# Two kinds of DMA writes change places between ScalarE's queue and SyncE's

## The chip, the cores and the metric

The kernel runs on one core of a Trainium2 chip. The metric is the device time of one execution in microseconds, the median of several; lower is better.

## The reference

The program is linear attention followed by a layer of eight experts. For each of 8 batches and 8 heads, `kv = k^T v` (64 x 64) over 576 positions, `out = q kv`, and each row of 64 is divided by its root mean square and multiplied by `g_norm`. The heads side by side are the rows `x` (4608 tokens x 512). Then

```python
logits = x @ w_gate
e_idx = argmax(logits, axis=1)
gate_w = probs[arange(N), e_idx]            # softmax of logits
eom = sigmoid(x @ w_output_gate)
for e in range(8):
    mask = e_idx == e
    h = maximum(x[mask] @ w1[e], 0)         # 512 -> 1024
    out[mask] = gate_w[mask, None] * eom[mask, e, None] * (h @ w2[e])
```

All of it is float32; the kernel splits float32 operands of the large products into a high and a low part.

## The kernel before

**Tiles and groups.** The 4608 tokens are 36 tiles of 128. Tiles 0 to 15 are the early ones (`EARLY = 16`), 16 to 35 the late ones. They also form four groups of 9, 7, 10 and 10 tiles (`GR`); the first two groups are the early tiles. `kv_part` makes a batch's kv product (kvps, L586), `kvT_part` and `m_part` fold the gate weights into it, `out_tile` multiplies a tile's q with it (ops, L665) and evicts the result: on ScalarE the raw row `xrow` (L674), the squares `sq` (L677) and the gate sums `gp` (L696). Two tiles share one row buffer of 512 KB. When the second of the pair is evicted, `write()` sends the buffer to DRAM (`xs`) through `xwrite` (L1064), 18 times in all: 8 for early tiles and 10 for late ones.

**Row buffers.** Loads of k, v and q (L549) and row buffers of the late part come from one pool of eight slots, `xfree`. `load` fills it with loads until one slot is left. `take` hands out the slot that has been free longest, and `give` puts a slot back as soon as its write has been issued; the next user waits for that write to land.

**Norms and routing.** `route` runs once for each group: the inverse norms of the rows (`xtail`, L760), the logits, the argmax, the rank of each token in its expert, and the tables of token numbers. `xtail` holds 16 numbers a token, eight inverse norms and one scale for the output. The early groups write their norms at once to `xr` (L763, L765). The rest of their scales, `rest_of_scales`, is left for later: the first layer steps it three times (at f = 1, 2, 3), and its third step issues the write of `xtail` to `xt` on ScalarE's queue (L865), for both early groups. The late groups write theirs through `xwrite`.

**Experts.** `run(i)` does one layer pass: `mm1` in eight blocks f (hps, L405: 12 matmuls each), whose result ScalarE evicts with a Relu (hT, L413) and VectorE makes a low part of (L415); two buffers of hps alternate, so block f + 2 waits for VectorE's work on block f. Then `mm2` for each tile of 128 tokens (yps, L441: 24 matmuls), evicted with the output scale from `tl` (y, L453) and scattered to `out` (L454). Weights are loaded in pieces of 512 KB on SyncE's queue (wraw, L220, `wload`) and split on ScalarE (whi, L256 and L263) and VectorE (wlo, L259 and L266). GpSimd gathers token rows (`xg`) and their norms and scales (`tl`, L283) by index. The first eight passes use early tokens only (256 for each expert), the later ones the rest.

**Order.** The order on every engine and queue is written out by hand (`manual_schedule`). Work of the late tiles is a generator, `late`, of which one step is taken after each block of a layer (`unit`); so kvps, ops and their evictions stand between the blocks of the first passes. `early()` is the time up to the first layer, about 66 us. After it `late_open[0]` is set to True and the first late pair (tiles 16 and 17) is finished; the pairs after it follow in the first passes, up to about 190 us. In the first pass, the block f = 3 is followed by the weights' load `wload(1, 1, 1)`, then by the third step of `rest_of_scales` and then by a step of `late`.

**Queues.** SyncE's queue issues all loads and all rows; ScalarE's queue stands in ScalarE's own order of instructions, so a DMA issue that must wait holds all of ScalarE's work behind it.

Of the kernel before, what the change touches and what calls it, by code (L numbers as in the profile page):

```python
# [153 lines left out]
def body(ctx: ExitStack, tc: tile.TileContext, kvm, rem, qT, wg, gn, w1, w2, kc, xs, xr0, xr, xt, tab, out):  # L154
    nc = tc.nc
# [35 lines left out]
    held = {}  # L191
# [8 lines left out]
    def give(t):  # L200
        i = held.pop(id(t))[0]
        (free if i < SLOTS else xfree).append(i)
# [73 lines left out]
    def rows_of(dram, g0, n):  # L276

        r0, w, t = (EARLY, EARLY, g0) if g0 < EARLY else (XE, LATE, g0 - EARLY)
        return dram[r0:r0 + P * w].rearrange("(m s) x -> m s x", s=w)[:, t:t + n]
# [140 lines left out]
    def mm2(i, k, events):  # L420
# [31 lines left out]
        else:  # L452
# [21 lines left out]
    xtail = c1.tile([P, NT, TW], F32, name="xtail")  # L474
# [3 lines left out]
                        in_=xtail[:, 0:w // TW, :].rearrange("p n x -> p (n x)"))  # L478
# [29 lines left out]
    for i in range(2):  # L508
        o = c1.tile([P, GMAX + 1, E], BF16, name=f"ohb{i}")
# [129 lines left out]
    def out_tile(g, later=False):  # L639
# [45 lines left out]
        def write():  # L685
            xwrite(c0, rows_of(xs, c0, k), x)
# [35 lines left out]
    def route(gi):  # L722
# [5 lines left out]
        n = len(GROUPS[gi])  # L728
        last = gi + 1 == len(GROUPS)
        g0 = GROUPS[gi][0]  # L730
# [30 lines left out]
        rows_ = rows_of(xt, g0, n)  # L761
# [8 lines left out]
        def scaled(j):  # L770
            w = j.stop - j.start
            eng = nc.gpsimd if gi < EARLY_GROUP and j.start else vec
            eng.tensor_tensor(out=gpv[:, :, j], in0=gpv[:, :, j],
                              in1=rv.unsqueeze(2).to_broadcast([P, n, w, E]), op=ALU.mult)

        def summed(j):
            return vec.tensor_reduce(out=lg[:, :n, j], in_=gpv[:, :, j], axis=AX.X, op=ALU.add)
# [50 lines left out]
        def gate():  # L828
            vec.tensor_tensor(out=og[:, :n], in0=oh[:, :n], in1=lg[:, :n, E:2 * E], op=ALU.mult)
            yield 0  # L830
            vec.tensor_reduce(out=ogs[:, :n], in_=og[:, :n], axis=AX.X, op=ALU.add)
            yield 0
            vec.tensor_scalar(out=ogs[:, :n], in0=ogs[:, :n], scalar1=-88.0, scalar2=None, op0=ALU.max)

        def exps():
            nc.scalar.activation(ex[:, :n], d[:, :n], AF.Exp)
            nc.scalar.activation(eo[:, :n], ogs[:, :n], AF.Exp, scale=-1.0)

        def norm(k):
            if k == 0:  # L840
                vec.tensor_reduce(out=se[:, :n], in_=ex[:, :n], axis=AX.X, op=ALU.add)
            elif k == 1:
                vec.tensor_scalar(out=eo[:, :n], in0=eo[:, :n], scalar1=1.0, scalar2=None, op0=ALU.add)
            else:
                vec.tensor_scalar(out=se[:, :n], in0=se[:, :n], scalar1=1e-9, scalar2=None, op0=ALU.add)

        def scales():
            vec.reciprocal(dn[:, :, :n], dn[:, :, :n])
            yield 0
            vec.tensor_tensor(out=xtail[:, g0:g0 + n, C_SCALE], in0=se[:, :n], in1=eo[:, :n], op=ALU.mult)  # L850

        def rest_of_scales():
            if lead:
                scaled(halves[1])
                summed(halves[1])
            for _ in gate():
                pass
            yield
            exps()
            for k in range(3):  # L860
                norm(k)
            for _ in scales():
                pass
            yield
            nc.scalar.dma_start(out=rows_, in_=xtail[:, g0:g0 + n])  # L865
            yield

        early = g0 < EARLY
# [113 lines left out]
        if not early:  # L982
            yield from scales()
            xwrite(g0, rows_, xtail[:, g0:g0 + n])
# [27 lines left out]
        elif not lead:  # L1012
            tps, acc = table_part(0, TMAX)
            yield from pause(9)
            if not gi:
                nc.scalar.copy(gix0, tps[:, 0, 0:1])
                gather_row(0, 0)
            vec.tensor_copy(acc, tps)
            scales_late.append(rest_of_scales())
        else:  # L1020
            tps, acc = table_part(0, TA, rl)
# [15 lines left out]
            tick[0] = None  # L1037

            scales_late.append(rest_of_scales())

            def others():
# [13 lines left out]
    issued = []  # L1055
    issue_mark = c1.tile([P, 1], F32, name="issue_mark")
    xwrites = []
    opened = [False]

    def xwrite(g, o, i):  # L1060
        if not opened[0]:
            xwrites.append((g, o, i))
            return
        nc.sync.dma_start(out=o, in_=i)  # L1064
        if id(i) in held:
            give(i)

    def open_rows():
        opened[0] = True
        for w in list(xwrites):  # L1070
            xwrite(*w)
        xwrites.clear()
# [195 lines left out]
            step()  # L1268
            yield

    late_open = [False]
    vec = nc.vector
    ce = cf[:, K_E:K_E + E]
    perm = cst.tile([P, E, E], F32, name="perm")
# [257 lines left out]
    with ExitStack() as p3:  # L1532
# [4 lines left out]
        with tc.For_i(0, nreg) as i:  # L1537
# [36 lines left out]
            for f in range(8):  # L1574
                ph = pt.tile([P, P], F32, name="oph")
                for d in range(4):
                    o = d * 256 + (f % 2) * P
# [3 lines left out]
            for f in range(8):  # L1581
# [5 lines left out]
                                         in_=y, in_offset=None, bounds_check=NTOK - 1, oob_is_err=False)  # L1587


def build():  # L1590
    nc = bacc.Bacc("TRN2", target_bir_lowering=False, num_devices=1)

    def inp(name, shape, dt=F32):
        return nc.dram_tensor(name, shape, dt, kind="ExternalInput").ap()

    kvm = inp("kvm", (B, P, 4, 2, DM))
    rem = inp("rem", (B // 2, P, 2, DM))
    qT = inp("qT", (NTOK // QC, P, NP, QC))
    wg = inp("wg", (P, 2, 4 * E))
    gn = inp("gn", (P, 1))  # L1600
    w1 = inp("w1", (E, 4, P, 1024))
    w2 = inp("w2", (E, 4, P, 1024))
    kc = inp("kc", (P, K_N))
    out = nc.dram_tensor("out", (NTOK, DM), F32, kind="ExternalOutput").ap()
    xs = nc.dram_tensor("xs", (XR, DM), F32).ap()
    xr0 = nc.dram_tensor("xr0", (XE, TW), F32).ap()
    xr = nc.dram_tensor("xr", (XE, TW), F32).ap()
    xt = nc.dram_tensor("xt", (XR, TW), F32).ap()
    tab = nc.dram_tensor("tab", (P, NOVER), F32).ap()
    with tile.TileContext(nc) as tc:  # L1610
        body(tc, kvm, rem, qT, wg, gn, w1, w2, kc, xs, xr0, xr, xt, tab, out)
    return nc
# [27 lines left out]
```

## Time and profile before

| what | us |
|---|---|
| median of 3 runs (582.49 to 587.55) | 582.75 |
| the profiled execution's own time | 582.92 |
| its span, first to last instruction | 581.0 |
| TensorE busy in the span | 557.4 |
| VectorE, ScalarE, GpSimd busy | 344.3, 286.2, 221.6 |
| mean granted TensorE clock | 0.994 |

The time is the span and about 2 us around it. Rows of the profile name an engine (PE is TensorE, PEld its weight loads, DVE is VectorE, ACT is ScalarE, POOL is GpSimd, SP is SyncE; a q behind the name means that the engine's sequencer issues or waits), a line of the kernel, an operation, and what it writes and reads. A granted clock of 1.00 is 2.4 GHz and 0.50 is 1.2 GHz.

### The profile page before, as it was taken

Reading aid. Unit: us, or ns where it says so; the run is one execution under the profiler, and the core shown is the slowest. Engines: PE = TensorE matmul, PEld = TensorE weight load, DVE = VectorE, ACT = ScalarE, POOL = GpSimd, SP = SyncE. Lnnn points to the kernel's source line nnn. Section 1 sums busy time; section 2 is a strip of 40 time slices with the busy share of each in tenths; the row PEclk is TensorE's granted clock in tenths of the full one; section 3 lists DMA queues with packets and bytes.
Section 4 is the critical chain, followed back from the end, with each engine's and each line's share of the span. In section 5 each row is a group of like instructions: output and inputs, shape, how many; then the busy total and the mean of one; then the engine's idle time right before and its main releaser. Section 6 shows DMA issues by size and latency. Waiting matters only on the chain.

```text
span 581.0 us, 11889 instructions
## 1 busy us (share of the span) xinstructions
PE 557.4 (96%) x4643; PEld 478.0 (82%) x4643; DVE 344.3 (59%) x635; ACT 286.2 (49%) x486; POOL 221.6 (38%) x204
## 2 busy tenths in 40 slices
PE   7998997999999999999999999999999999999995
PEld 3775786898988898888979889889897988888894
DVE  2268555565587989877595746445355363646450
ACT  1355346566666656746563434535344444535440
POOL 4343333332313251533565326235262453545202
PEclk9999999999999999999999999999999999999998
DMA  8999799986966485666855445346454645556200
GB/s 306 418 417 368 244 415 361 321 309 248 313 221 232 157 307 199 197 231 207 273 188 195 130 146 156 118 152 211 146 179 142 202 162 156 176 170 207 75 6 38
DMA packets 38794, 126.31 MB, mean 217 GB/s; under 512 B 6940, under 2 KB 8333, under 8 KB 38736
## 3 DMA queue, kind: packets, MB, share of 16 engines
q1 hardware_dynamic: 29664, 105.26, 52.5%
q0 software_dynamic: 8352, 19.88, 10.1%
q8 instruction: 38, 0.62, 0.4%
q10 hardware_dynamic: 720, 0.39, 0.2%
q14 instruction: 20, 0.16, 0.1%
HBM read 106.01 MB, written 20.04 MB: 217 GB/s over the span
## 4 chain that ended last, share of the span: by engine, by line
PE 76%; DMA 9%; DVE 5%; issue 4%; ACT 3%; POOL 1%; ACTq 0%; POOLq 0%; SPq 0%; DVEq 0%
PE hps L405 32%; PE yps L441 31%; PE ops L665 4%; DMA ld<-qT 3%; DMA ld<-kvm 3%; PE tps L350 3%; PE yps L435 3%; PE kvps L586 2%; DVE wlo L266 2%; DMA wgs<-wg 1%; ACT whi L263 1%; PE cps L558 1%; DVE wlo L259 1%; DVE hT L415 1%; DMA xs<-xrow 1%
## 5 line engine op out<-in xcount | busy, mean ns | idle before, releaser
L405 PE MATMUL hps<-xT,whi 128*128 128x256 f32 (+8 forms) x992 | 214.2, 308 | 3.6 <-DVE hT L415 2.2
L441 PE MATMUL yps<-whi,hT 128*128 128x512 f32 (+3 forms) x592 | 200.7, 402 | 0.0
L405 PEld LDWEIGHTS hps<-xT,whi 128*128 128x128 f32 x992 | 163.9, 190 | 10.1 <-DVE hT L415 3.9
L405 PE MATMUL hps<-xT,wlo 128*128 128x256 f32 (+8 forms) x496 | 150.8, 304 | 0.0
L441 PEld LDWEIGHTS yps<-whi,hT 128*128 128x128 f32 (+3 forms) x592 | 111.0, 187 | 24.5
L441 PE MATMUL yps<-wlo,hT 128*128 128x512 f32 (+3 forms) x296 | 116.7, 394 | 0.0
L415 DVE SCALAR_TENSOR_TENSOR hT<-hps,hT 128x256 fp32r<-128x256 f32 (+9 forms) x168 | 62.9, 394 | 90.5 <-ACT hT L413 81.1
L454 POOL DMA_INDIRECT out<-y,oidx x42 | 45.5, 1084 | 178.2 <-ACT y L453 143.2
L413 ACT ACTIVATE hT<-hps 128x256 fp32r<-128x256 f32 (+8 forms) x128 | 55.1, 430 | 116.0 <-PE hps L405 107.8
L259 DVE SCALAR_TENSOR_TENSOR wlo<-wraw,gcol,whi 128x1024 fp32r<-128x1024 f32 x62 | 83.4, 1347 | 44.6 <-ACT whi L256 43.0
L266 DVE TENSOR_TENSOR wlo<-wraw,whi 128x1024 fp32r<-128x1024 f32 x64 | 84.3, 1317 | 25.7 <-ACT whi L263 22.3
L405 PEld LDWEIGHTS hps<-xT,wlo 128*128 128x128 f32 x496 | 94.0, 189 | 0.3
L256 ACT ACTIVATE whi<-wraw,gcol 128x1024 fp32r<-128x1024 f32 x62 | 71.3, 1151 | 0.6 <-DVE wlo L266 0.6
L317 POOL TENSOR_TENSOR xg<-xg,tl 128x512 f32<-128x512 f32 (+8 forms) x41 | 48.3, 1178 | 54.3 <-DMA tl<-xt,gidx 39.6
L283 POOL DMA_INDIRECT xg<-xs,gidx x41 | 46.7, 1140 | 53.6 <-PE hps L405 33.1
L263 ACT CAST whi<-wraw 128x1024 fp32r<-128x1024 f32 x64 | 66.6, 1041 | 0.0
L283 POOL DMA_INDIRECT tl<-xt,gidx x41 | 53.3, 1300 | 30.1 <-PE hps L405 18.3
L441 PEld LDWEIGHTS yps<-wlo,hT 128*128 128x128 f32 (+3 forms) x296 | 55.6, 188 | 10.4
L453 ACT ACTIVATE y<-yps,tl 128x512 f32<-128x512 f32 (+3 forms) x37 | 25.4, 687 | 60.3 <-PE yps L441 48.3
L353 ACT CAST xT<-tps 128x512 fp32r<-128x512 f32 (+8 forms) x42 | 23.0, 548 | 44.6 <-PE tps L350 43.5
L357 DVE TENSOR_TENSOR xT<-tps,xT 128x512 fp32r<-128x512 f32 (+8 forms) x42 | 26.6, 636 | 20.4 <-ACT xT L353 20.1
L665 PE MATMUL ops<-aug,ld 64*64 64x80 f32 (+1 forms) x960 | 32.1, 244 | 3.8 <-ACT gp L696 3.0
(184 smaller groups left out, 444.3 us busy)
## 6 DMA issues: line engine op xcount, KB each, us to landing
wraw<-w SPq DMA_DIRECT2D x128, 512.0 KB
ld<-kvm SPq DMA_DIRECT2D x32, 512.0 KB
ld<-qT SPq DMA_DIRECT2D x18, 512.0 KB
xs<-xrow SPq DMA_DIRECT2D x18, 512.0 KB
ld<-rem SPq DMA_DIRECT2D x4, 512.0 KB
out<-y,oidx POOLq DMA_INDIRECT x42
xg<-xs,gidx POOLq DMA_INDIRECT x41
tl<-xt,gidx POOLq DMA_INDIRECT x41
```

Source lines behind the costliest of these rows:

```text
L256: he.activation(hi, r, AF.Copy, scale=gcol[:, 0:1])
L259: eng.scalar_tensor_tensor(out=lo, in0=r, scalar=gcol[:, 0:1], in1=hi.bitcast(F32), op0=ALU.mult, op1=ALU.subtract)
L263: he.copy(hi, r)
L266: eng.tensor_tensor(out=lo, in0=r, in1=hi.bitcast(F32), op=ALU.subtract)
L283: return nc.gpsimd.indirect_dma_start(out=o[:M, :], out_offset=None, in_=dram[0:XE] if i < E else dram, in_offset=bass.IndirectOffsetOnAxi ...
L317: return eng.tensor_tensor(out=v, in0=v, in1=f, op=ALU.mult)
L405: seq.append(nc.tensor.matmul(ps[:, :C], w[:, o:o + P], x[d][:, :C], start=(d == 0 and k == 0), stop=(d == 3 and k == 2)))
L413: nc.scalar.activation(h[:, 0:C], ps[:, :C], AF.Relu)
L415: nc.vector.scalar_tensor_tensor(out=h[:, l:l + b - a], in0=ps[:, a:b], scalar=0.0, in1=h[:, a:b].bitcast(F32), op0=ALU.max, op1=ALU.subtract)
L441: seq.append(nc.tensor.matmul(ps[:M], a, b, start=(f == 0 and n == 0), stop=(f == 7 and n == 2)))
L454: i_ = nc.gpsimd.indirect_dma_start(out=out, out_offset=bass.IndirectOffsetOnAxis(ap=oidx[i // E][:M, RUNS[i][0], t:t + 1], axis=0), in_=y ...
L665: nc.tensor.matmul(ps[c0:c0 + step_, u, p * W:(p + 1) * W], qt[g // 2][r, p, q0:q0 + step_], augs[b % 3][r, p, :], start=True, stop=True)
```

## The change

The third step of `rest_of_scales` issues its write on SyncE's queue instead of ScalarE's (two writes, one for each early group). `xwrite` asks two things: has `late_open` been set, and is the tensor in the table `held` of slots that are in use. If both hold, the write goes on ScalarE's queue, else on SyncE's as before. `late_open` is made earlier in the text, since `xwrite` now reads it. Nothing else differs: the order of the steps, the slots and the data stay.

```diff
@@ rest_of_scales @@
             yield
-            nc.scalar.dma_start(out=rows_, in_=xtail[:, g0:g0 + n])
+            nc.sync.dma_start(out=rows_, in_=xtail[:, g0:g0 + n])
             yield
@@ before xwrite @@
-    opened = [False]
+    opened, late_open = [False], [False]
 
     def xwrite(g, o, i):
         if not opened[0]:
             xwrites.append((g, o, i))
             return
-        nc.sync.dma_start(out=o, in_=i)
+        (nc.sync if late_open[0] is False or id(i) not in held else nc.scalar).dma_start(out=o, in_=i)
         if id(i) in held:
             give(i)
@@ after late @@
-    late_open = [False]
     vec = nc.vector
```

## Rows read from the trace of the kernel before

**Rows 1.** The page's first part: busy us, share of the span, instructions.
```profile
PE 557.4 (96%) x4643; PEld 478.0 (82%) x4643; DVE 344.3 (59%) x635; ACT 286.2 (49%) x486; POOL 221.6 (38%) x204
```

**Rows 2.** Stretches: length, busy us of PE, PEld, DVE, ACT, POOL, clock, DMA, GB/s.
```profile
80.00:90.00 10.00, 7.77 (x114) 6.59 (x109) 4.79 (x16) 4.26 (x10) 3.13 (x4) 1.00 0.99 382
90.00:100.00 10.00, 7.35 (x96) 5.90 (x97) 5.21 (x9) 5.33 (x12) 4.45 (x3) 0.98 1.01 368
...
99.00:104.00 5.00, 5.00 (x45) 3.99 (x38) 4.26 (x6) 4.82 (x8) 0.94 (x1) 0.66 0.97 387
110.00:180.00 70.00, 70.00 (x941) 60.83 (x940) 44.88 (x78) 43.73 (x83) 18.82 (x18) 1.00 0.79 277
```

**Rows 3.** TensorE's waits, 66 to 112 us: total us, times, longest.
```profile
PE kvps L586 <- issue: 1.1, 3, 0.4
```

**Rows 4.** TensorE's timeline: start, us, instructions, idle time before and its releaser.
```profile
88.23 0.50 PE L405 MATMUL hps<-xT,whi 128*128 128x256 f32 x2 [1.12 <-DVE hT L415]
...
90.90 0.51 PE L405 MATMUL hps<-xT,whi 128*128 128x256 f32 x2
...
98.75 0.79 PE L665 MATMUL ops<-aug,ld 64*64 64x80 f32 x32 [2.40 <-ACT gp L696]
```

**Rows 5.** ScalarE's timeline, from the first late pair to the first layer's end.
```profile
72.71 0.42 ACT L696 COPY gp<-ops 128x128 f32<-128x128 f32 x1
...
85.04 2.25 ACTq L865 DMA_DIRECT2D xt<-xtail  x2
87.33 0.38 ACT L413 ACTIVATE hT<-hps 128x256 fp32r<-128x256 f32 x1 [3.60 <-PE hps L405]
...
97.33 0.58 ACT L674 COPY xrow<-ops 128x512 f32<-128x512 f32 x1 [3.04 <-DMA xs<-xrow]
...
104.70 1.14 ACT L256 ACTIVATE whi<-wraw,gcol 128x1024 fp32r<-128x1024 f32 x1
```

**Rows 6.** The chain that ended last, 72 to 112 us: start, us, what.
```profile
73.48 11.48 DMA ld<-qT
```

**Rows 7.** SyncE's timeline: DMA issues from 67 to 104 us.
```profile
67.37 0.33 SPq L220 DMA_DIRECT2D wraw<-w  x1
67.77 1.30 SPq L549 DMA_DIRECT2D ld<-kvm  x2
69.19 3.46 SPq L220 DMA_DIRECT2D wraw<-w  x4
73.48 0.33 SPq L549 DMA_DIRECT2D ld<-qT  x1
75.36 0.33 SPq L1064 DMA_DIRECT2D xs<-xrow  x1
76.53 0.33 SPq L549 DMA_DIRECT2D ld<-qT  x1
77.80 0.33 SPq L220 DMA_DIRECT2D wraw<-w  x1
...
89.52 0.39 SPq L1064 DMA_DIRECT2D xs<-xrow  x1
...
92.33 4.06 SPq L220 DMA_DIRECT2D wraw<-w  x3
102.14 0.33 SPq L1064 DMA_DIRECT2D xs<-xrow  x1
```

**Rows 8.** Line L865: its instructions, ns min/median/max, first and last start.
```profile
L865 ACTq DMA_DIRECT2D xt<-xtail x2: 336/338/341, 85.0 to 86.9; - x2
```

**Rows 9.** GpSimd's timeline: gathers of norms and what waits for them.
```profile
79.20 0.94 POOL L283 DMA_INDIRECT tl<-xr,gidx  x1 [2.27 <-PE hps L380]
...
85.17 1.05 POOL L317 TENSOR_TENSOR xg<-xg,tl 128x512 f32<-128x512 f32 x1 [3.77 <-DMA tl<-xr,gidx]
...
93.37 0.99 POOL L283 DMA_INDIRECT tl<-xt,gix  x1 [0.15 <-PE kvTps L604]
```

**Rows 10.** TensorE's waits, 112 to 232 us: total us, times, longest.
```profile
PE ops L665 <- ACT gp L696: 0.6, 1, 0.6
```

## The prediction

> **What bounds the kernel now.** I read the page's busy times first, then the busy time by stretch, then TensorE's waits, then the chain and the queues at those places.
>
> TensorE is busy for 557.4 of 581.0 us [rows 1]: a change of queues can only give back idle time, or time at the lower clock. By stretch [rows 2], the reader is to see that 80 to 104 us is the weak place: TensorE is busy for 7.77 and 7.35 us of two stretches of 10, and then full at a lower clock; 110 to 180 us is full, at 1.00. The DMA share is near 1 at the weak place. Of the idle 4.88 us (2.23 + 2.65), 1.1 are unnamed waits of kvps [rows 3]; 1.12 us before hps at 88.23 are ended by VectorE's hT, and 2.40 before ops at 98.75 by ScalarE's gp [rows 4]; 0.26 are left in small gaps. Behind the 2.40 us the clock falls: from 99 to 104 us its mean is 0.66 [rows 2], so 5 x 0.34 = 1.70 us of work at 2.4 GHz are lost.
>
> Both idle times come from ScalarE, and both touch the change [rows 5]. At 85.04 its queue issues the two L865 writes, and hT L413, whose matmuls were over, starts at 87.33 after 3.60 us of idle time. At 97.33 the row copy L674 has waited 3.04 us for DMA xs<-xrow: the row buffers are run down to one spare, so a new pair of tiles gets the buffer that the pair before has just been written from, and waits for that write to land.
>
> Why L865 waits: the chain [rows 6] has a qT load ahead of it, issued at 73.48 and landed 11.48 us later, though L865 reads no qT. I read that an issue on either queue waits for the landing of the eighth issue before it. On SyncE's timeline [rows 7] qT of 73.48, the row write of 75.36, qT of 76.53 and the weights of 77.80 come one after the other, then four loads and the two L865; the first L865 has qT of 73.48 as its eighth in the program's order, the second the row write of 75.36. The second L865 goes at 86.95 (85.04 + 2.25 - 0.34, [rows 5, 8]), so landings come 1.9 us apart there, some 11 us behind their issue.
>
> **The two L865 writes go to SyncE's queue.** Removed from ScalarE: the 3.60 us. The fifth block's hT comes at about 84.1 instead of 87.33, and the 1.12 us before the seventh go, with the small gaps behind them. Added to SyncE: two issues of 0.34 us [rows 8] with the same kind of wait; behind them on that queue are loads, and no TensorE wait in this stretch is put down to a load. Cost there 0; if the loads came to be late, each held issue would cost TensorE up to the 1.9 us of one landing.
>
> What is late next is the norms' landing. They have landed by 93.37 now, when GpSimd's gather tl<-xt goes [rows 9]. Issued at some 85 us behind SyncE's backlog, they land at about 95. A gather of this kind took 5.97 us (79.20 to 85.17, [rows 9]), so tl lands at 101; ScalarE's y, which stands just ahead of the split at 104.70 [rows 5], would want it at about 100. That is a wait of 1 to 1.5 us on ScalarE while TensorE has the next tile's matmuls in the other buffer: cost 0, or some 2 us if the gather is 5 us later than I think.
>
> **The ten late row writes go to ScalarE's queue.** It is all ten: the flag is set before tile 17 is evicted, and their buffers are in the table that the new condition asks. The late groups' norms are not, and stay on SyncE.
>
> First, a write no longer stands behind SyncE's backlog. The second pair's took 7.8 us (89.52 to 97.33, [rows 5, 7]). 512 KB at the 368 to 387 GB/s of the stretch are 1.4 us, so 3 if it shares the engines with loads; between 3 and 7.8 I take 4, since its queue is empty. ScalarE comes to the next row copy at 93 to 94; a write issued by 90 has landed. So the 2.40 us go, and with them, likely, the 1.70 of the clock. Bounds: nothing of it (the write lands as late as now), or all 4.10.
>
> Second, the issue now stands in ScalarE's order with its wait. Queued behind it: hT, the split of w2, the next row; VectorE's hT waits for these, and TensorE for VectorE, two blocks later. Pair one is ready at 73.1 [rows 5]; its eighth issue before is the weights of 67.37, which released SyncE's row write at 75.36, or the load just ahead of them: held 2.2 us or 0. Of 2.2 us the 1.1 of unnamed idle time at 80 us would swallow half. I take 0, as ScalarE is ahead of SyncE here. Pair two counts: ready at about 86.8, its eighth issue before is qT of 76.53 in today's order, which lands at about 88.5 by the spacing of 1.9; if SyncE, no longer held by the row, comes one load ahead of it, it is the weights of 77.80, at 90.2. Held 1.7 or 3.4 us. Freed at 88.5 it costs the layer's last block, which would start at 89.3, nothing; freed at 90.2, 1.4 us. I take 0.5, nearer to today's order, and 0.4 for VectorE's kvc and the transposes behind the same wait. Pairs three to ten are free: the third is written at 102.14 [rows 7], 14 us behind its eighth, and landings took under 12.
>
> Third, ten issues of 0.34 us on ScalarE. From 110 to 180 us TensorE is busy for all 70.00 us with ScalarE at 43.73 [rows 2]: cost 0, and 2 us if none of it were covered. Beyond that, one wait for gp of 0.6 us [rows 10] lies near three issues: 0 to 1 us, I take 0.3. SyncE is rid of its waits for rows; weights come earlier, but TensorE does not wait for them: 0.
>
> **The sum.** 1.12 + 0.26 + 2.40 + 1.70 = 5.48 us gained, 0.5 + 0.4 + 0.3 = 1.2 given back: 4.3 us. From the profiled execution's 582.92 (span 581.0 and 1.9 around it) that gives 578.6; it is 0.17 above the median of the three runs, 582.75, so 578.5.
>
> The Trainium skill (DMA: Bandwidth & Descriptors, Issuing engines are not separate DMA queues) says that DMAs from SP, ACT and GpSimd run on the same 16 engines, so that spreading them saves issue time only. The trace agrees that they are full, at shares of 0.97 to 1.01. By that rule the row writes would bring nothing; the sum counts on the latency of one write, and not on rate.
>
> **Rivals.** *DMA is the bound.* What jumps the queue delays what it passes, and the next layer's weights land when they land. For: ScalarE's split at 104.70 uses weights issued at 92.33 [rows 5, 7], which land at 100 to 104 by the 7.8 and 11.48 us seen, so little can be gained at that point. Against: TensorE needs that split only at the next layer's fifth block. If it holds ScalarE, and the transposes behind it, some 1.7 us remain: 581.0; at the worst, nothing: 582.7. The skill's rule above is this rival.
>
> *ScalarE is held*, the slower side: the wait of pair two. If the eighth issue before is two or three loads further on, it lands at 92 to 94. This decides from 90.1 on: if ScalarE is freed later, the last block starts after its present 90.90 [rows 4], and each us costs TensorE one. Freed at 93 it starts at 93.8, 2.9 us late; kvc's chain adds 1.3, the clock falls as now, and of the savings 2.40 us stay: 584.5. Held to 97, with pair one held too, 588 to 589. For: a 3.60 us wait of this kind stands in the trace. Against: the order of issue, by which pair two counts back to a load made 10 us before.
>
> *The change doesn't do what it says:* with the row writes still on SyncE's queue, only L865's 1.38 us would go: 581.4. The code speaks against it.
>
> **How the numbers follow.** Forecast 0.57, its own range 577.2 to 580.3. DMA bound (with late tails and the change without effect) 0.18, at 581.0 to 582.7. ScalarE held 0.14, of which 0.07 above 588.6. More than 5.8 us gained, for which the 1.1 us at 80 us or waits behind 180 would have to go too, 0.11, at 576 to 577. The range 576.6 to 584.5 leaves out the long end of the held case and some of the last. A measurement of this kernel tells about 1% (5.8 us) from no change: faster by more 0.11, slower by more 0.07, within 0.82.
>
> **What would show it.** Right: no idle time of 2 us on ScalarE between 83 and 88; row writes that land within 5 us; no idle TensorE before ops at 94 to 98, and a granted clock of 1.00 from 99 to 104; everything behind 110 us some 4 us earlier. Wrong: ScalarE held for 3 us at the second row write, y waiting for tl, or the lower clock still there. If the stretches behind 110 us are no longer full, the loss is one I have not seen.

## The result, and the profile after

Before: 582.75 us, median. After: 590.3 us (589.48 to 592.15, five runs). The ratio is 1.0115, with a 95% interval of 1.0085 to 1.0144: slower by 1.15%, and clear of no change. Medians are of all runs and ratios of the runs as a whole without those in a slower state, some per cent longer at a lower granted clock, so that a ratio is not the quotient of two medians (here 1.0130). The profiled execution has a span of 588.4 us against 581.0, so 7.4 us are to be explained.

The stretches of [rows 2] and some behind them (columns as there), after the change:

```profile
70.00:80.00 10.00, 9.53 (x166) 9.13 (x170) 5.88 (x15) 5.83 (x15) 2.16 (x2) 1.00 1.00 389
80.00:90.00 10.00, 8.92 (x164) 7.78 (x156) 5.92 (x16) 4.36 (x11) 4.45 (x4) 1.00 1.03 415
90.00:100.00 10.00, 6.20 (x71) 4.90 (x63) 4.66 (x7) 5.09 (x10) 4.45 (x3) 1.00 1.03 416
...
99.00:104.00 5.00, 4.76 (x49) 3.85 (x50) 3.97 (x5) 5.00 (x10) 1.22 (x1) 1.00 0.97 296
110.00:180.00 70.00, 64.66 (x820) 55.86 (x819) 38.06 (x62) 38.12 (x73) 16.87 (x16) 0.95 0.70 246
...
130.00:140.00 10.00, 9.07 (x77) 7.17 (x78) 5.94 (x7) 6.61 (x14) 0.94 (x1) 0.83 0.74 260
160.00:170.00 10.00, 8.06 (x102) 7.33 (x102) 4.59 (x8) 6.64 (x15) 3.04 (x3) 0.83 0.65 242
```

The weak place gave nothing back in idle time: from 80 to 100 us TensorE is idle for 1.08 + 3.80 = 4.88 us, as before to the hundredth. Only the clock came back: 1.00 from 99 to 104 us, where it had been 0.66, worth the 1.70 us. The loss is where the row of before was full: from 110 to 180 us TensorE is idle for 70 - 64.66 = 5.34 us, and the clock has a mean of 0.95, which is 0.05 x 70 = 3.5 us of work, half of it in each of the two stretches at 0.83. With 0.47 us of idle time at 70 to 80 us the account is 5.34 + 3.5 + 0.47 - 1.70 = 7.6 us, for 7.4 measured.

TensorE's timeline after (columns as in [rows 4]) shows the idle times that fill most of this:

```profile
92.51 0.50 PE L405 MATMUL hps<-xT,whi 128*128 128x256 f32 x2 [2.40 <-DVE hT L415]
...
99.24 0.78 PE L665 MATMUL ops<-aug,ld 64*64 64x80 f32 x32 [1.03 <-ACT gp L696]
...
130.93 0.78 PE L665 MATMUL ops<-aug,ld 64*64 64x80 f32 x32 [3.28 <-ACT gp L696]
...
162.87 1.23 PE L665 MATMUL ops<-aug,ld 64*64 64x80 f32 x32 [1.94 <-ACT gp L696]
```

ScalarE's timeline after says why:

```profile
91.23 0.33 ACTq L1064 DMA_DIRECT2D xs<-xrow  x1
91.61 0.38 ACT L413 ACTIVATE hT<-hps 128x256 fp32r<-128x256 f32 x1 [4.16 <-DMA ld<-qT]
...
97.82 0.59 ACT L674 COPY xrow<-ops 128x512 f32<-128x512 f32 x1 [1.67 <-DMA xs<-xrow]
...
120.60 0.33 ACTq L1064 DMA_DIRECT2D xs<-xrow  x1
...
129.51 0.59 ACT L674 COPY xrow<-ops 128x512 f32<-128x512 f32 x1 [4.49 <-DMA xs<-xrow]
...
161.45 0.59 ACT L674 COPY xrow<-ops 128x512 f32<-128x512 f32 x1 [3.74 <-DMA xs<-xrow]
```

Two things are to be seen. At 91.23 the second pair's write holds ScalarE until a qT load lands: 4.16 us with the issue itself. It is the wait that stood at L865 in [rows 5], moved. And at 129.51 and 161.45 a row copy waits 4.49 and 3.74 us for the write before it, which has a queue of its own and was issued at once. In the chain of waits after (start, us, what) these writes are long:

```profile
72.98 6.94 DMA xs<-xrow
...
80.16 10.99 DMA ld<-qT
91.23 6.51 DMA xs<-xrow
...
120.60 8.84 DMA xs<-xrow
...
153.10 8.27 DMA xs<-xrow
```

What differs about the fourth pair's write (120.60) is best seen in SyncE's queue around it. Before the change, SyncE's timeline:

```profile
118.80 0.42 SPq L220 DMA_DIRECT2D wraw<-w  x1
121.62 0.33 SPq L1064 DMA_DIRECT2D xs<-xrow  x1
122.05 1.24 SPq L549 DMA_DIRECT2D ld<-kvm  x2
123.38 1.95 SPq L220 DMA_DIRECT2D wraw<-w  x2
```

and after it:

```profile
117.75 0.43 SPq L220 DMA_DIRECT2D wraw<-w  x1
118.27 1.91 SPq L549 DMA_DIRECT2D ld<-kvm  x2
120.28 1.42 SPq L220 DMA_DIRECT2D wraw<-w  x2
```

The four loads behind the row are the same. Before, SyncE stands for some 2.4 us (119.2 to 121.62) until the row is copied, issues it, and only then the loads. After, it goes on, and three of the four loads are out when ScalarE's queue issues the row at 120.60. The row copy of before that needs this write's buffer waits little for it, in ScalarE's timeline:

```profile
126.52 0.59 ACT L674 COPY xrow<-ops 128x512 f32<-128x512 f32 x1 [0.47 <-DMA xs<-xrow]
```

So the write took 126.52 - 121.62 = 4.9 us behind a queue that had paused, and 8.84 us on an empty queue beside one that had not.

The trace also has the packets of each DMA queue by stretch: packets, MB, and their share of the 16 engines. q1 is SyncE's queue, q10 ScalarE's and q0 GpSimd's. After the change, from the issue at 120.60 to 125.20 us:

```profile
q1 hardware_dynamic: 379, 1.39, 96.6%
```

and from 125.24 us until the write lands at 129.44:

```profile
q1 hardware_dynamic: 255, 0.95, 55.1%
q10 hardware_dynamic: 144, 0.52, 30.5%
q0 software_dynamic: 112, 0.27, 16.2%
```

The first packet of the write moves 4.64 us after the issue. Until then the engines move the loads of SyncE's queue; after it the queues share the engines for 4.2 us. More than half of the 8.84 us is the wait for the first packet. ScalarE's queue is not slow by itself: the writes that it issued at 180.44 and 194.24, when SyncE's queue had next to nothing under way, had their first packet after 0.84 and 0.83 us and their last after 2.53 and 2.45.

SyncE's waits before the change, 60 to 200 us (total us, times, longest), sum these pauses:

```profile
SPq L1064 <- ACT xrow L674: 39.9, 8, 6.7
```

They were not time that the loads could win. After the change SyncE stands no less in all, but most of it at the buffers of the weights and of the loads. At these two places it had been 7.2 and 7.9 us:

```profile
SPq L220 <- DVE wlo L266: 27.3, 6, 7.9
...
SPq L220 <- DVE wlo L259: 13.2, 4, 6.6
```

The loads behind a row leave a few us earlier, just ahead of its write, and then wait elsewhere.

### The profile page after: what moved, and what is told of

Its sections match the earlier page's. It is cut to its first block, busy times and chain, and to the rows that moved or that the text cites. A ratio compares the mean times of both kernels' runs of the same rounds, so it can differ in the third digit from the quotient of the medians.

```text
span 588.4 us, 11884 instructions
## 1 busy us (share of the span) xinstructions
PE 559.9 (95%) x4643; PEld 479.6 (82%) x4643; DVE 343.5 (58%) x635; ACT 286.5 (49%) x486; POOL 217.1 (37%) x204
## 4 chain that ended last, share of the span: by engine, by line
PE 75%; DMA 11%; DVE 5%; issue 4%; ACT 3%; POOL 1%; POOLq 0%; ACTq 0%; SPq 0%
PE yps L441 31%; PE hps L405 30%; DMA xs<-xrow 5%; PE ops L665 4%; PE tps L350 3%; PE yps L435 2%; PE kvps L586 2%; DMA ld<-qT 2%; DVE wlo L266 2%; DMA ld<-kvm 1%; DMA wgs<-wg 1%; PE cps L558 1%; ACT whi L263 1%; DMA tl<-xr,gidx 1%; ACT xrow L674 1%
## 5 line engine op out<-in xcount | busy, mean ns | idle before, releaser
L317 POOL TENSOR_TENSOR xg<-xg,tl 128x512 f32<-128x512 f32 (+8 forms) x41 | 45.5, 1110 | 52.5 <-DMA tl<-xt,gidx 38.3
L283 POOL DMA_INDIRECT tl<-xt,gidx x41 | 51.0, 1244 | 28.0 <-PE hps L405 18.2
```

The costliest lines, as they stand in the source:

```text
L283: return nc.gpsimd.indirect_dma_start(out=o[:M, :], out_offset=None, in_=dram[0:XE] if i < E else dram, in_offset=bass.IndirectOffsetOnAxi ...
L317: return eng.tensor_tensor(out=v, in0=v, in1=f, op=ALU.mult)
```

## The experiments

Theory one, the **backlog**: SyncE's waits for rows had kept the loads behind each row; without them the loads are ahead of the write on the DMA engines, on whatever queue it is. Its rival, **ScalarE held**: the issue in ScalarE's order holds ScalarE, and the rest follows from that. A second rival is that the **norms** on SyncE's queue do the harm. Ratios are to the kernel before on the same chip.

**One part alone.** The first kernel has the norms on SyncE's queue and all rows there too, the second the late rows on ScalarE's queue and L865 as before.

```diff
@@ norms_only, of the changed kernel @@
-        (nc.sync if late_open[0] is False or id(i) not in held else nc.scalar).dma_start(out=o, in_=i)
+        nc.sync.dma_start(out=o, in_=i)
@@ rows_only, of the changed kernel @@
-            nc.sync.dma_start(out=rows_, in_=xtail[:, g0:g0 + n])
+            nc.scalar.dma_start(out=rows_, in_=xtail[:, g0:g0 + n])
```

> Only the two L865 writes go to SyncE's queue; all rows stay there too. Theory (backlog: with the rows on ScalarE's queue SyncE no longer waits for them, issues loads ahead of them, and the writes land 6.5 to 8.9 us after their issue, so the next pair waits for its row buffer): this part is no cost. ScalarE's 3.60 us of idle time at 85 us go, the 1.12 us of TensorE too, the wait for ops near 98 us stays: 580 to 582 us. Rival (late norms: the gather of tl waits for norms behind SyncE's backlog and ScalarE's y waits for it): 583 us or more, with a ScalarE wait for tl near 100 us.

> Only the late rows go to ScalarE's queue; L865 stays there too. Backlog theory: the idle times before ops near 128 and 161 us of the changed kernel (3.28 and 1.94 us) and the two stretches of 3.4 us at half the clock are all there: 589 to 593 us. Rival (ScalarE held: the 4.16 us at the second row write are the cause): with L865 ahead of it the second write counts back to another issue, so its hold changes by over 1 us, and the time follows that hold and not the stalls near 128 and 161.

Norms alone: 584.96 us, ratio 1.0002 [0.9972, 1.0031], above the 580 to 582 us expected, and without the wait for tl that its rival named. Rows alone: 592.25 us, 1.0131 [1.0089, 1.0174], as expected and all of the loss. The norms on SyncE's queue do no harm, but bring nothing either, though ScalarE's 3.60 us and TensorE's 1.12 us of [rows 4, 5] are gone. SyncE's and ScalarE's timelines of the kernel with the norms alone say where that went:

```profile
88.83 0.86 SPq L865 DMA_DIRECT2D xt<-xtail  x2
90.37 0.54 SPq L1064 DMA_DIRECT2D xs<-xrow  x1
```

```profile
97.92 0.59 ACT L674 COPY xrow<-ops 128x512 f32<-128x512 f32 x1 [6.82 <-DMA xs<-xrow]
```

The second pair's row leaves SyncE's queue at 90.37, no earlier than the 89.52 of [rows 7], and the copy that waits for it starts 0.6 us later. ScalarE is ready for the buffer 3.2 us earlier (91.10 against 94.29) and waits 3.8 us longer (6.82 against 3.04).

In the kernel with the rows alone, ScalarE's hold at the second pair is 1.98 us instead of 4.16, but 3.82 us at L865 are back ahead of it, so ScalarE is held no less in all, and this run does not decide about that rival. TensorE's waits at 128 and 160 us are there (3.14 and 2.15 us). Its profiled execution shows no stretch at the lower clock there, so the clock's part differs between executions; the idle time doesn't.

**SyncE held again.** The rows stay on ScalarE's queue, but the first load behind each of them waits until the row has been copied, as SyncE's own issue had to.

`behind(d, x)` makes d wait for x; the issues of `wload` and `load` are wrapped in `held_back`, and `last_row` remembers the row copy L674.

```diff
@@ sync_held, of the changed kernel @@
+    hold = [None]
+
+    def held_back(d):
+        if hold[0] is not None:
+            behind(d, hold[0])
+            hold[0] = None
+        return d
...
-            nc.sync.dma_start(out=t, in_=src)
+            held_back(nc.sync.dma_start(out=t, in_=src))
...
-        (nc.sync if late_open[0] is False or id(i) not in held else nc.scalar).dma_start(out=o, in_=i)
+        on_act = late_open[0] and id(i) in held
+        (nc.scalar if on_act else nc.sync).dma_start(out=o, in_=i)
+        if on_act:
+            hold[0] = last_row[0]
```

> The changed kernel, but the first load that SyncE issues behind each late pair waits for that pair's second row copy, as SyncE did when it issued the row itself. Backlog theory: the fourth and sixth writes land in under 5.5 us instead of 8.84 and 8.27, the idle times before ops near 128 and 161 us fall below 0.7 us, the clock stays at 2.4 GHz there: 581 to 585 us. Rival (ScalarE's own queue is slow, whatever SyncE does): the writes still take 6.5 to 9 us, and the time stays at 588 us or above. Rival (ScalarE held): the hold of about 4 us at the second write stays, and with it 588 us or above.

581.76 us, as expected, ratio 0.9954 [0.9922, 0.9986], and 1.6% below the changed kernel's ratio, with the queue of every write as the change has it. ScalarE's timeline, and then TensorE's waits from 66 to 200 us:

```profile
90.06 0.33 ACTq L1074 DMA_DIRECT2D xs<-xrow  x1
90.44 0.38 ACT L421 ACTIVATE hT<-hps 128x256 fp32r<-128x256 f32 x1 [3.72 <-DMA wraw<-w]
...
119.41 0.36 ACTq L1074 DMA_DIRECT2D xs<-xrow  x1
...
125.83 0.59 ACT L682 COPY xrow<-ops 128x512 f32<-128x512 f32 x1 [2.00 <-DMA xs<-xrow]
```

```profile
PE ops L673 <- ACT gp L704: 2.4, 3, 1.0
PE hps L413 <- DVE hT L423: 2.0, 1, 2.0
```

The fourth pair's write now lands 6.4 us after its issue (125.83 - 119.41), not 8.84, though not in the 5.5 us expected; its first packet moves after 1.60 us, not 4.64. TensorE's waits for gp fall to 2.4 us in all. ScalarE is held for 3.72 us at the second pair, nearly as long as in the changed kernel, and the loss is gone all the same: that speaks against ScalarE held. So these waits of SyncE's queue are worth some 9 us (1.6% of 590.3). The landing is slower than the 4.9 us of the kernel before, probably because here SyncE's first load leaves at the same moment as the write (119.41).

**The second pair's write alone on SyncE's queue.** This takes ScalarE's long hold away and leaves the other nine.

```diff
@@ pair2_sync, of the changed kernel @@
-        (nc.sync if late_open[0] is False or id(i) not in held else nc.scalar).dma_start(out=o, in_=i)
+        (nc.sync if late_open[0] is False or id(i) not in held or g == 18 else nc.scalar).dma_start(out=o, in_=i)
```

> The changed kernel with the second late pair's write alone left on SyncE's queue, so that ScalarE is not held behind it. Backlog theory: ScalarE's 4.16 us of idle time and TensorE's 2.40 us near 90 us go, the idle times near 128 and 161 us and the lower clock stay: 586 to 589 us. Rival (ScalarE held is the cause): 584 us or less.

591.92 us, ratio 1.0138 [1.0076, 1.02], above the 586 to 589 us expected and further from the rival's 584. The hold is gone and the next row copy waits 4.95 us for the buffer in its place, as with the norms alone; the waits at 128 and 162 us stay (3.13 and 1.83 us). ScalarE's hold is not what makes the change slow.

**One more spare row buffer.** The late write's landing matters only if somebody waits for the buffer. `load` is to leave two slots free instead of one, in the changed kernel, in the kernel before and in the one with the norms alone.

```diff
@@ after_spare2, before_spare2, norms_spare2 @@
-    load(late_loads, xfree, 1)
+    load(late_loads, xfree, 2)
```

> The changed kernel with loads stopping at two free slots instead of one, so that a pair's row buffer is not the one that the pair before has just been written from. Backlog theory (the late landing hurts only through that buffer): the writes of 6 to 9 us stay, but ScalarE's waits for xs<-xrow go, and with them TensorE's idle times near 98, 128 and 161 us and both stretches at the lower clock; the 2.40 us near 90 stay: 579 to 582 us. Rival (the deeper backlog hurts in other ways too, late loads or weights): 585 us or more, with TensorE or ScalarE waiting for loads.

> The kernel before with loads stopping at two free slots. Backlog theory: the 2.40 us before ops near 98 us and the stretch at the lower clock go (4.1 us), the 1.12 us behind L865 stays: 578 to 580.5 us. Rival (one load less in flight costs as much as the buffer gives): 582 us or more, with kvps or ops waiting for loads.

> Only the two L865 writes on SyncE's queue, rows on SyncE's queue, and loads stopping at two free slots. Backlog theory: what the L865 part won, and what was lost again in the wait for the row buffer (5.08 us and 6.83 us at half the clock in its own run), is kept: 576 to 579 us, about 1.4 us below the kernel before with two free slots. Rival (the norms land late and hold y): no faster than that kernel.

583.7 us (1.0027 [1.0002, 1.0053]), 583.85 (1.0025 [0.9996, 1.0054]) and 583.82 (1.0043 [1.0019, 1.0066]): with a spare more it makes no difference that these intervals show which queue writes the rows. All three missed their ranges. In the changed kernel the wait at 127 us is gone, which speaks for ScalarE's waits for rows as the way in which the late landings cost time. It is no gain, for the loads come later by one slot: in the kernels with all rows on SyncE's queue TensorE now waits 4.33 and 4.67 us at kvps for a load, and in the changed one 2.44 us at 154 us for gp again, and ScalarE 6.02 us at the second pair for qT. The test is not a clean one for that reason, since it moves loads too.

**The rows on SyncE's queue, behind the loads.** If the backlog is the cause and not ScalarE's queue, rows that SyncE issues behind its loads must be as slow. Each late row is put aside and sent on SyncE's queue at the end of the next weights' load, or before the next pair takes its row buffer; no late row is on ScalarE's queue.

```diff
@@ loads_first, of the changed kernel @@
         raw[(i, which, c)] = r
+        send_rows()
         return d
+
+    late_rows = []
+
+    def send_rows():
+        while late_rows:
+            o_, i_ = late_rows.pop(0)
+            nc.sync.dma_start(out=o_, in_=i_)
...
         if not chunk:
+            send_rows()
...
-        (nc.sync if late_open[0] is False or id(i) not in held else nc.scalar).dma_start(out=o, in_=i)
+        if late_open[0] and id(i) in held:
+            late_rows.append((o, i))
+            give(i)
+            return
+        nc.sync.dma_start(out=o, in_=i)
```

> No late row on ScalarE's queue: all are written on SyncE's, but each write is issued behind the loads and the one weights' load that follow it in the kernel before, so that these no longer wait for the row. L865 on SyncE's queue, as in the change. Backlog theory: what costs is the loads ahead of a write, on whatever queue the write is; the fourth pair's write lands later than in the kernel before, ScalarE waits 1 to 4 us for xs<-xrow near 128 us, and the time is 586 to 591 us. Rival (a write on ScalarE's own queue is slow by itself): writes land as in the kernel with L865 alone moved, no wait near 128, 583 to 585 us.

600.67 us, ratio 1.0325 [1.0299, 1.0352], far above the 586 to 591 us expected. In the chain of waits:

```profile
81.44 12.93 DMA xs<-xrow
...
134.23 8.58 DMA xs<-xrow
...
164.67 9.79 DMA xs<-xrow
```

The writes take 8.58 and 9.79 us on SyncE's own queue, like the 8.84 and 8.27 of the changed kernel on ScalarE's. Loads that stand ahead of a row cost it on this queue too, and the queue on which it goes does not decide. The size of the loss overstates this: the second row is issued only at 99.64 here, 8 us later than in the changed kernel, and TensorE's longest wait (13.1 us, for gp) contains that.

**Getting more from it.** With SyncE held, ScalarE's 3.72 us at the second pair are left. The next two kernels send that row, or all ten, on GpSimd's queue.

```diff
@@ pair2_pool, of sync_held @@
-        (nc.scalar if on_act else nc.sync).dma_start(out=o, in_=i)
+        (nc.gpsimd if on_act and g == 18 else nc.scalar if on_act else nc.sync).dma_start(out=o, in_=i)
@@ pool_rows, of sync_held @@
-        (nc.scalar if on_act else nc.sync).dma_start(out=o, in_=i)
+        (nc.gpsimd if on_act else nc.sync).dma_start(out=o, in_=i)
```

> The kernel in which SyncE is held for the rows as before, with the second pair's write on GpSimd's queue and the other nine on ScalarE's. Theory: ScalarE's hold of 3.72 us behind that write and TensorE's 1.96 us near 90 go, and the write, issued at 87 instead of 90, lands before the next row copy wants its buffer: 1.5 to 3.5 us less than the held kernel, a ratio of 0.990 to 0.994 to the kernel before. Rival (the hold was covered by the weights' landing anyway): the same 0.995 as the held kernel, with the idle time somewhere else before 112 us.

> SyncE held for the rows as before, and all ten late writes on GpSimd's queue. Theory: as the kernel with the second pair alone there, 0.990 to 0.994; ScalarE issues nothing. Rival (GpSimd is held for each row, and gathers and the scaling of rows behind it come late): above 1.000, with TensorE waiting for xg or ScalarE for tl.

One row: 579.45 us, ratio 0.9981 [0.9955, 1.0008], no more than with SyncE held alone. All ten: 584.67 us, 1.0049 [1.0029, 1.0068]. Neither came to the 0.990 to 0.994 expected. With all ten, GpSimd waits in its own order for rows, in its waits over the span:

```profile
POOL xs L1074 <- ACT xrow L682: 23.5, 8, 7.0
```

and TensorE's waits for gp are back at 124 and 155 us (2.56 and 2.79 us). With one row, GpSimd's timeline shows it leave at once, and the next limit:

```profile
85.37 0.62 POOL L1074 DMA_DIRECT2D xs<-xrow  x1
...
96.58 0.98 POOL L291 DMA_INDIRECT tl<-xt,gix  x1 [2.47 <-DMA xt<-xtail]
```

The row left 4.7 us before the 90.06 of ScalarE's queue, the idle time of 2.0 us at hps is gone (1.5 us stand at 86.6 us instead, before ops), and the gather of the norms is late, having waited 2.47 us for L865's writes on SyncE's queue. ScalarE's y at 102.58 waits 3.38 us for tl, and TensorE 0.38 + 1.06 us for the xT behind it.

So the norms go to GpSimd's queue as well, and, as a control, the norms alone go there in the kernel before.

```diff
@@ norms_pool, of pair2_pool; rows_before_norms_pool, of the kernel before @@
-            nc.sync.dma_start(out=rows_, in_=xtail[:, g0:g0 + n])
+            nc.gpsimd.dma_start(out=rows_, in_=xtail[:, g0:g0 + n])
```

(In the kernel before, the line removed is ScalarE's.)

> The kernel with SyncE held for the rows and the second pair's write on GpSimd's queue, and now the two L865 writes on GpSimd's queue too. Theory: off SyncE's backlog the norms land by 90 us, so the gather of tl is not held, ScalarE's 3.38 us of idle time ahead of y and TensorE's 1.44 us near 105 go: 1 to 2 us less, a ratio of 0.992 to 0.996 to the kernel before. Rival (GpSimd's own writes push its gathers back by as much, or the idle time returns at the next row buffer): 0.998 or above.

> The kernel before with the two L865 writes alone moved, to GpSimd's queue instead of SyncE's; all rows on SyncE's queue. Theory: as with L865 on SyncE's queue the hold of ScalarE goes and the wait for the row buffer near 95 us takes the time back, as that write is paced by SyncE's backlog: 0.998 to 1.003. Rival (on SyncE's queue the norms themselves pushed that row write back): faster than the kernel before by 0.4% or more.

All together: 578.46 us (577.88 to 581.23), ratio 0.9925 [0.9902, 0.9947], as expected, and faster than the kernel before and the changed one (from SyncE held alone, at 0.9954, the intervals don't tell it apart). Its profiled execution is the longest of the six, 581.23 us. GpSimd's timeline there:

```profile
86.30 0.57 POOL L1074 DMA_DIRECT2D xs<-xrow  x1
...
95.58 1.02 POOL L291 DMA_INDIRECT tl<-xt,gix  x1 [0.15 <-issue]
```

The gather no longer waits, and y waits 0.92 us for tl instead of 3.38. The control gives 584.24 us, 1.0009 [0.9993, 1.0024], with a row wait of 8.01 us on ScalarE at 98.60: the same as the norms on SyncE's queue, and as expected. Taking ScalarE's 3.60 us away is worth nothing by itself on either of the two queues.

## Why the prediction was wrong

The forecast was 578.5 us, in a range of 576.6 to 584.5; 590.3 is outside it, on the side that had a chance of 0.07.

*"First, a write no longer stands behind SyncE's backlog ... between 3 and 7.8 I take 4, since its queue is empty."* This step failed. The writes took 6.51 to 8.84 us where a row copy or the chain shows it. An empty queue says when a DMA is issued, not when the engines that all queues share come to it: at the fourth pair 4.64 us later, while 1.39 MB of loads went ahead. I had set the Trainium skill's rule aside with the words that the sum counts on latency and not on rate; here the rate at which the loads moved made the latency. The runs with SyncE held and with the loads first show it from both sides.

*"SyncE is rid of its waits for rows; weights come earlier, but TensorE does not wait for them: 0."* and *"From 110 to 180 us ... cost 0."* Here lies most of the error. I asked who waits for the loads that come earlier, and not what they collide with. The 39.9 us in which SyncE waited for rows looked like a cost of before; they were what kept the engines free for each row. Priced at 0 with an end of 2 us, this stretch lost 8.8 us.

*"Held 1.7 or 3.4 us ... I take 0.5."* The second pair held ScalarE for 4.16 us with the issue. By the 1.9 us of the prediction's own spacing the two landings would have been 88.9 and 90.8, not 88.5 and 90.2. SyncE's timeline after the change shows what was ahead of that write:

```profile
77.80 0.33 SPq L220 DMA_DIRECT2D wraw<-w  x1
80.16 2.41 SPq L549 DMA_DIRECT2D ld<-qT  x2
84.02 0.33 SPq L220 DMA_DIRECT2D wraw<-w  x1
84.40 1.30 SPq L865 DMA_DIRECT2D xt<-xtail  x2
87.37 2.60 SPq L549 DMA_DIRECT2D ld<-kvm  x3
```

Counted back from 91.23 these are three loads of k and v, two L865, one of weights and two of qT: the eighth is the qT of 80.16, which landed at 91.15 by the chain. The way of counting was right, and the order was not: SyncE, no longer held by the row, had gone two loads further than I took it to have, past the qT of 76.53 and the weights of 77.80. That is the rival of ScalarE held, and by its own point (90.1 us) it decides: TensorE came to its block at 92.51, for the 90.90 of before, and its 2.40 us moved from gp to hT. But the rival was not the cause of the loss behind 110 us: the kernel without the hold is no faster than the change, and the one with SyncE held keeps 3.72 us of it and has no loss.

*"1.12 + 0.26 + 2.40 + 1.70 = 5.48 us gained."* Net of the waits that came in their place, only the 1.70 came. Waits here stand one behind the other: with the norms off ScalarE's queue, the next row copy waits for its buffer by at least as much as was gained.

*What is late next is the norms' landing*: right, and priced too low. In the changed kernel it doesn't show, for the gather at 95.24 came right behind other work of GpSimd. With the second pair's row on GpSimd's queue the norms landed at 95.81 by the chain, where about 95 was said, and cost 3.38 us on ScalarE and 1.44 on TensorE, for 1 to 1.5 and 0.

*DMA is the bound*, at most no gain by the prediction, was nearest to the truth, and priced too low: what jumps the queue can also be overtaken.

The last sentence of the prediction, on the stretches behind 110 us, named the place as one where I saw no loss. The account of it is closed for the idle time and the clock (7.6 us for 7.4). Open is why the first packet of a write on ScalarE's queue comes 3.4 to 4.6 us after its issue when loads stand ahead of it on SyncE's; no run takes the reason apart.

## What to carry to other kernels

A queue that waits for a late producer does two jobs: it orders its own DMAs, and it keeps the ones behind it off the shared engines. Before a write is moved to an idle queue to free the other, look at what that queue will issue in the time won, and whether its bytes go ahead of the write on which somebody waits. If so, keep the order with an explicit dependency, and price each wait that goes by the wait behind it.

## What the hardware showed that I had not expected

A write of 512 KB alone on its queue took 8.84 us beside four loads that another queue issued from 118.27 to 121.70. From 125 to 130 us the changed kernel's DMA moved 384 GB/s, at which the write alone is 1.4 us. The Trainium skill (DMA: Bandwidth & Descriptors, Queues, rings and completion order) has each engine take turns between queues, packet by packet. By equal turns with one other queue the write would be an estimated 2.7 us at this rate. Once its packets move, the trace agrees: from 94.65 to 97.30 us the second pair's 0.52 MB moved beside 0.59 MB of SyncE's queue, at shares of 48.3 and 54.4%. But that write was issued at 91.23, and its first packet came 3.42 us later; the fourth pair's came after 4.64. Turns between packets don't give the landing, 6.3 to 8.8 us where a row copy waited for it, and the measurement decides.

The hold on an issue reaches over both queues: ScalarE's issue at 91.23 waited for a load of SyncE's queue, while GpSimd's at 85.37, in the kernel with one row there, waited for none. The traces name the semaphore that tells of each DMA's landing. All issues of SyncE's and ScalarE's queues share eight of these, and GpSimd's row has another; in the changed kernel 181 of the 203 issues that have an eighth before them in time carry the same one as it. So the hold goes with eight semaphores used in turn, as far as the traces tell, and not with a queue; no run changed their number.

TensorE's 2.40 us of idle time ahead of 98.75 were followed by a granted clock of 0.66 in the five us behind [rows 2, 4], and its 2.40 us ahead of 92.51 after the change by 1.00. The same idle time doesn't always cost the clock, and it is not to be counted as sure.
